# Gated mix of an S5 scan and a SiLU MLP on one core: later columns of the first x rows in two loads, the third block of W1 on ScalarE's queue, the parameter rows on SyncE's queue

## The chip, the cores and the metric

The kernel runs on one core of a Trainium2 chip. The metric is the device time of one execution in microseconds (us). Before the change three executions took 137.16, 136.59 and 137.13 us; their median is 137.13 us. One execution was also taken with the hardware profiler: it took 137.01 us.

## The reference

x has 2048 rows of 448 numbers in bf16, and so has the output. Per row a gate g = sigmoid(sum(x * gate_w)) mixes two branches, `g * a + (1 - g) * b`:

```
a:  Lam_bar = exp(exp(log_dt) * (Lambda_re + 1j*Lambda_im))
    Bu = x @ (((Lam_bar - 1)/Lam)[:, None] * (B_re + 1j*B_im)).T
    h_t = Lam_bar * h_{t-1} + Bu_t                  # 2048 steps
    a = 2 * real(h @ (C_re + 1j*C_im).T) + x * Dskip
b:  b = silu(x @ w1) @ w2                           # 448 -> 1792 -> 448
```

## The kernel before

The 2048 rows of x are read as 1024 pairs, `x2` (line 160): a pair of rows, the even and the odd one, lies in one row of 896 numbers. The work goes by quarters of 512 rows (even or odd, first or second half). The MLP's first product needs x with its columns on the partitions: 448 columns are three blocks of 128 (j = 0, 1, 2) and a rest of 64 (j = 3). W1 lies in `W1E` in the same four blocks. TensorE (PE) runs the MLP's first product into PSUM, ScalarE (ACT) applies SiLU from PSUM to `AT`, and PE runs the second product with W2. Between these, PE makes Bu, VectorE (DVE) runs the scan, and at the end PE applies C.

A small tracker (lines 43 to 148) records every operation with the tiles it reads and writes, derives the semaphore waits, and emits the instructions of each engine in recorded order. So each engine, and each of the two queues that issue DMAs (SyncE's, SP in the profile, and ScalarE's, ACTq), works strictly in the order of the code. All plain loads are issued through one helper, line 226.

The change lies in the start-up, before the steady state:

- **Loads** (lines 275 to 300). Only the first quarter (even rows, first half: 512 pairs in four row blocks k = 0 to 3) has its x brought in plain form, into `XH`, which is a view of the tile `XN`. Its columns 0 to 255 (j = 0, 1) come in four loads of 64 KB, keys XA0 to XA3. Its columns 256 to 511 (j = 2 and the rest) come in one load of 256 KB for all four row blocks, key XB, on ACT's queue (line 284). W1's columns 0 to 767 come by row block: block 0 in two halves, block 1 (192 KB, line 281) and block 2 (192 KB, line 285) on SP's queue. Three parameter rows of 0.9 KB, log_dt, Lambda_re and Lambda_im, go to three partitions of the tile `R` (`ld_row`, line 261); two are on SP's queue and Lambda_im is on ACT's. Then follow the rest of block 3 (`ld_wr`), the other columns of W1, the gate and skip vectors.
- **Transposes by DMA** (lines 307 to 318). SP waits until both `ld_wr` loads have landed (`gE`), and then issues transposing DMAs for the other quarters of x and for B.
- **PE's first work** (lines 484 to 522). After 22 warm-up products PE turns the first quarter itself, 128x128 at a time, against an identity (`turn_x`, line 488); DVE copies the result from PSUM to `XT` (`turned_x`, line 496). The generator `ffn1_first` (line 426) gives the first products (line 432) of six output blocks: all that need j = 0, then j = 1, then j = 2, broken off at fixed places. The order on PE is: turns of j = 0 and 1 for row blocks 0 and 1; products of j = 0; turns of j = 0 and 1 for blocks 2 and 3 among them; three products of j = 1; `mm_cols` (line 468), which turns the parameter rows in `R` into columns; the turns of j = 2; three more products of j = 1; the turns of j = 3; six products of j = 2; then `ffn1_rem` (line 442) with the rest of 64 columns, and after it the pairs of line 364.
- **Parameters**. DVE copies a stripe of `R` (`rd`, line 464), then PE's `mm_cols` result to `PV` (line 514). ACT and DVE form from it dt, the decay magnitude and the angles (lines 551 to 584).
- **Later uses of x**. The gate and the skip product (lines 632 to 647) read the whole of `XH` and wait for all keys in the list `XA`.

Of the kernel before, what the change touches and what calls it, by code (L numbers as in the profile page):

```python
# [150 lines left out]
def gated_mix(nc, A_x, A_Lambda_re, A_Lambda_im, A_B_re, A_B_im, A_C_re, A_C_im, A_log_dt,  # L151
              A_Dskip, B_x, B_w1, B_w2, gate_w, out):
    with ExitStack() as ctx:
        E = ctx.enter_context
        T = Tracker(nc, ctx)

        def sb(name, shape, dtype):
            return E(nc.sbuf_tensor(name, list(shape), dtype))
# [30 lines left out]
        ID = sb("ID", [128, 128], BF16)  # L189
# [31 lines left out]
        ps = E(nc.psum_tensor("ps", [128, 8, 512], F32))  # L221
# [3 lines left out]
        def ld(eng, dst, src, key, group=None):  # L225
            return T.dma(eng, lambda e: e.dma_start(dst, src), writes=[key], group=group)  # L226
# [23 lines left out]
        def row(v):  # L250
            return v.rearrange("(o n) -> o n", o=1)

        XH = XN[:, 0:8 * D].rearrange("p (k c) -> p k c", k=4)
        XA = ["XA0", "XA1", "XA2", "XA3", "XB"]
        FA, FB = 768, 1280
        x0 = x2[0:512, 0:512].rearrange("(k p) c -> p k c", p=128)

        def ld_w(eng, j, f0=0, f1=FA, key=""):
            ld(eng, W1E[:, j, f0:f1], B_w1[j * 128:(j + 1) * 128, f0:f1], f"W1Ej{j}{key}")

        def ld_row(eng, i, v):
            ld(eng, R[i:i + 1, 0:D], row(v), f"R{i}", gR if i < 2 else gR2)
# [5 lines left out]
        def ld_wr(eng, c, later):  # L268
            p = slice(64 * c, 64 * c + 64)
            if later:  # L270
                return ld(eng, W1E[p, 3, 384:896].rearrange("p (n f) -> p n f", n=2),
                          B_w1[384:448, FA:].rearrange("p (n c f) -> p n c f", n=2, c=2)[:, :, c, :], f"W1Es{c}")
            return ld(eng, W1E[p, 3, 0:384], B_w1[384:448, 384 * c:384 * c + 384], f"W1Er{c}")

        for k, eng in enumerate(("sp", "act")):
            ld(eng, XH[:, k, 0:256], x0[:, k, 0:256], XA[k])
        for c, eng in enumerate(("sp", "act")):
            ld_w(eng, 0, 384 * c, 384 * c + 384, c)
        for k, eng in ((2, "sp"), (3, "act")):
            ld(eng, XH[:, k, 0:256], x0[:, k, 0:256], XA[k])  # L280
        ld_w("sp", 1)
        for i, (eng, v) in enumerate((("sp", A_log_dt), ("sp", A_Lambda_re), ("act", A_Lambda_im))):
            ld_row(eng, i, v)
        ld("act", XH[:, :, 256:512], x0[:, :, 256:512], XA[4])
        ld_w("sp", 2)
        gE = [ld_wr(eng, c, False) for c, eng in enumerate(("sp", "act"))]
        ld_w3("sp", 0, 2, FA, FB, "d")
        ld_w3("act", 2, 3, FA, FB, "d")
# [23 lines left out]
        for i, src in enumerate((A_B_re, A_B_im)):  # L312
# [15 lines left out]
             writes=["IOTA"])  # L328
# [128 lines left out]
        def ffn1(c, f0=0, ahead=None):  # L457
            for fb in range(f0, NFB, 2):
                pair(*ffn1_pair(c, fb), last=(c == 3 and fb == NFB - 2))
                if ahead and fb == 8:  # L460
                    ahead()
                yield
# [22 lines left out]
        PB = (6, 7, 6, 7)  # L485
        xp = [ps[:, b, 0:256].bitcast(BF16) for b in PB]

        def turn_x(j, i):
            def mm(pe):
                ins = None  # L490
                for k in (2 * i, 2 * i + 1):
                    ins = pe.transpose(xp[j][:, k * 128:(k + 1) * 128], XH[:, k, j * 128:(j + 1) * 128], ID[:, :])  # L492
                return ins
            T.op("pe", mm, reads=(XA[2 * i:2 * i + 2] if j < 2 else [XA[4]]) + ["ID"], writes=[f"ps{PB[j]}"])

        def turned_x(j, i=None):
            c, key = (slice(0, 512), f"XTe0{j}") if i is None else (slice(256 * i, 256 * i + 256), f"XTe0{j}{i}")
# [2 lines left out]
        for j in range(2):  # L500
            turn_x(j, 0)
            turned_x(j, 0)
        warm(2, 5)
        first = ffn1_first()
        next(first)
        turn_x(0, 1)
        turned_x(0, 1)
        next(first)
        turn_x(1, 1)
        turned_x(1, 1)  # L510
        rd()
# [4 lines left out]
            reads=["pv", "ps7"], writes=["PV"])  # L516
# [30 lines left out]
        def pact(o, a, f, ra, scale=1.0, bias=0.0):  # L547
# [20 lines left out]
            reads=["f2"] + SGN, writes=["f2s"])  # L568
# [55 lines left out]
        def xblock(b):  # L624
            v = XN[:, 4 * b * D:4 * (b + 1) * D].rearrange("p (k c) -> p k c", k=4) if b > 1 else \
                XH[:, :, b * D:(b + 1) * D]
            return v, [*(XA if b < 2 else []), *([f"XN{b // 2}"] if b else [])]

# [12 lines left out]
        def skip():  # L641
            for b in range(4):
# [17 lines left out]
             writes=["BTz"] + BTK[2:4])  # L660
# [486 lines left out]
        f = ffn1(2)  # L1147
# [70 lines left out]
def bass_gated_mix__ssm_conv_s5__dense_activation_silu__prompt_kernel(nc, *args):  # L1218
    gated_mix(nc, *args)
# [28 lines left out]
```

## Time and profile before

| | |
|---|---|
| median of the three runs | 137.13 us (136.59 to 137.16) |
| profiled execution | 137.01 us |
| its span (first to last instruction) | 135.6 us |
| PE busy | 132.3 us, 98% of the span |
| DVE, ACT, POOL busy | 113.8, 93.7, 16.9 us |
| bytes by DMA | 11.95 MB, of them 10.53 MB on SP's queue (q1) and 1.27 MB on ACT's (q10) |

The profile page shows busy time by engine, then the span in 40 slices, the DMA queues, the chain of work that ended last, and groups of instructions by line. PEld is the loading of the stationary matrix, which overlaps PE. SPq and ACTq are the sequencers that issue DMAs. An issue is short; its bytes move later, on 16 DMA engines that both queues share. The views of the trace list single instructions with start and duration in us from the span's start, and after them, in brackets, how long the engine was idle before and what released it.

### The profile page before, as it was taken

The page shows a single profiled execution, that of the slowest core. Times are in us where ns is not written, and L with a number is a line of the kernel's source. Part 1 is how long each engine was busy: PE and PEld are TensorE (multiplying, and loading weights), DVE is VectorE, ACT ScalarE, POOL GpSimd, SP SyncE. Part 2 cuts the span into 40 slices and gives each one's busy share as a digit, 9 for nine tenths or more (in the row PEclk, how much of TensorE's full clock was granted, in tenths as well). Part 3 has the DMA queues.
Part 4 walks back from the last instruction along what each step waited for, and adds up shares of the span by engine and source line. Part 5 has one row for each costly group of instructions (what it writes and reads, how often), then busy time and mean ns, then how long its engine had stood idle before and what let it go on. Part 6 is the DMA issues. An engine that isn't in the chain of part 4 may idle for free.

```text
span 135.6 us, 2631 instructions
## 1 busy us (share of the span) xinstructions
PE 132.3 (98%) x1074; PEld 66.3 (49%) x1075; DVE 113.8 (84%) x150; ACT 93.7 (69%) x146; POOL 16.9 (12%) x32
## 2 busy tenths in 40 slices
PE   7989999999999999999999999999999999999993
PEld 7644444444444555444445544445555555555552
DVE  1358899917699998999999999999999999994554
ACT  0459888899939999778999597797213437879200
POOL 7107758550000000000000000000000000000000
DMA  3999969997899130000122000000000000222123
GB/s 115 255 288 184 156 137 249 172 291 256 234 223 132 36 82 0 0 0 0 42 50 68 5 0 0 0 5 0 0 0 0 0 0 6 100 87 82 68 79 124
DMA packets 24912, 11.95 MB, mean 88 GB/s; under 512 B 16579, under 2 KB 24390, under 8 KB 24902
## 3 DMA queue, kind: packets, MB, share of 16 engines
q1 hardware_dynamic: 22868, 10.53, 34.2%
q10 hardware_dynamic: 2034, 1.27, 3.4%
q8 instruction: 8, 0.13, 0.4%
q14 instruction: 2, 0.02, 0.0%
HBM read 5.51 MB, written 1.84 MB: 54 GB/s over the span
## 4 chain that ended last, share of the span: by engine, by line
PE 92%; DMA 4%; ACTq 1%; DVE 1%; issue 0%
PE ps L364 43%; PE ps L780 16%; PE ps L795 16%; PE ps L1033 15%; DMA XN<-in_A_x_dram 4%; PE ps L432 1%; ACTq L226 1%; DVE TMPS L1057 1%; PE ps L446 1%; PE ps L492 0%
## 5 line engine op out<-in xcount | busy, mean ns | idle before, releaser
L364 PE MATMUL ps<-XT,W1E 64*128 64x512 bf16 x325 | 41.3, 376 | 0.0
L454 ACT ACTIVATE AT<-ps 128x1024 bf16<-128x1024 f32 x28 | 28.2, 1019 | 7.4 <-PE ps L364 7.2
L364 PEld LDWEIGHTS ps<-XT,W1E 64*128 64x128 bf16 x325 | 16.9, 94 | 19.0 <-ACT AT L454 0.3
L364 PE MATMUL ps<-XT,BT 64*128 64x512 bf16 x156 | 22.4, 376 | 0.0
L795 PE MATMUL ps<-W,AT 64*128 64x448 bf16 x224 | 21.5, 349 | 0.0
L780 PE MATMUL ps<-W,AT 128*128 128x448 bf16 x112 | 21.4, 353 | 0.0
L780 PEld LDWEIGHTS ps<-W,AT 128*128 128x128 bf16 x112 | 10.9, 98 | 10.5 <-issue 0.4
L795 PEld LDWEIGHTS ps<-W,AT 64*128 64x128 bf16 x224 | 10.9, 94 | 10.4
L824 ACT ACTIVATE BT<-ps,GT 128x448 bf16<-128x448 f32 x8 | 5.1, 633 | 13.2 <-PE ps L780 13.2
L880 DVE SCALAR_TENSOR_TENSOR HS<-VE,P,ps 128x512 bf16<-128x512 bf16 (+1 forms) x13 | 9.6, 780 | 4.0 <-PE ps L364 4.0
L364 PEld LDWEIGHTS ps<-XT,BT 64*128 64x128 bf16 x156 | 8.1, 94 | 9.4 <-DVE HS L880 0.3
L924 DVE TENSOR_TENSOR_SCAN G<-P,Q 128x1024 f32<-128x1024 f32 (+1 forms) x6 | 11.4, 1922 | 0.0
L1033 PE MATMUL ps<-CO,VE 128*128 128x448 bf16 (+2 forms) x63 | 11.1, 332 | 0.0
L1033 PE MATMUL ps<-CO,HS 128*128 128x448 bf16 x56 | 11.1, 352 | 0.0
L364 PE MATMUL ps<-XR,W1E 64*128 64x512 bf16 x25 | 9.2, 376 | 0.0
L1033 PEld LDWEIGHTS ps<-CO,VE 128*128 128x128 bf16 x63 | 6.0, 98 | 4.8
L1033 PEld LDWEIGHTS ps<-CO,HS 128*128 128x128 bf16 x56 | 5.5, 98 | 5.1
L877 DVE TENSOR_TENSOR Q<-G,COS 128x2048 bf16<-128x2048 f32 (+1 forms) x4 | 7.0, 1756 | 0.1
L877 DVE TENSOR_TENSOR Q<-G,SIN 128x2048 bf16<-128x2048 f32 (+1 forms) x4 | 7.0, 1750 | 0.0
L842 ACT ACTIVATE VE<-ps 128x1024 bf16<-128x1024 f32 x6 | 6.1, 1020 | 1.2 <-PE ps L364 1.2
L844 ACT ACTIVATE ps<-VE,P 128x1024 f32<-128x1024 bf16 x6 | 6.7, 1118 | 0.2
L880 DVE SCALAR_TENSOR_TENSOR VE<-HS,P,FP 128x512 bf16<-128x512 bf16 (+1 forms) x7 | 6.6, 977 | 0.1
(122 smaller groups left out, 181.7 us busy)
## 6 DMA issues: line engine op xcount, KB each, us to landing
W<-in_B_w_dram SPq DMA_DIRECT2D x2, 784.0 KB, 6.3
XN<-in_A_x_dram SPq DMA_DIRECT2D x1, 896.0 KB, 6.1
out_dram<-OT SPq DMA_DIRECT2D x8, 112.0 KB, 1.7
out_dram<-TMPS SPq DMA_DIRECT2D x7, 112.0 KB, 1.7
HS<-HS SPq DMA_DIRECT2D x4, 128.0 KB, 2.3
W1E<-in_B_w_dram SPq DMA_DIRECT2D x2, 192.0 KB, 4.1
XN<-in_A_x_dram SPq DMA_DIRECT2D x1, 384.0 KB, 3.8
XN<-in_A_x_dram ACTq DMA_DIRECT2D x1, 256.0 KB, 4.8
```

Of the source, the lines that this page charges most:

```text
L226: return T.dma(eng, lambda e: e.dma_start(dst, src), writes=[key], group=group)
L364: ins = pe.matmul(ps[:, bank, :], w(p, j), xh(odd, h, j, p), start=start and j == js[0], stop=stop and j == js[-1], skip_group_check=seeded)
L454: T.op("act", lambda e: e.activation(a[:, fb:fb + n, :], ps[:, bank:bank + n, :], AF.Silu), reads=[f"ps{bank + i}" for i in range(n)], wri ...
L780: ins = pe.matmul(ps[:, bank, 0:D], a[:, fb, q * 128:(q + 1) * 128], W2[:, ff(fb), :], start=(first and fb == 0), stop=(fb == NFB - 1), sk ...
L795: ins = pe.matmul(ps[:, bank, 0:D], a[p, fb, q * 128:(q + 1) * 128], W2[p, ff(fb), :], start=(start and fb == 0), stop=(not start and fb = ...
L824: T.op("act", lambda e: e.activation(bs(tile), ps[:, bank, 0:D], AF.Copy, scale=sc), reads=[f"ps{bank}", "GT2" if h else "GRI"], writes=ks)
L842: T.op("act", lambda e: e.activation(VE[:, m:m + 2, hs], ps[:, b[0]:b[0] + 2, :], AF.Copy), reads=[f"ps{i}" for i in b], writes=vs)
L844: T.op("act", lambda e: e.activation(ps[:, o[0]:o[0] + 2, :], VE[:, m:m + 2, hs], AF.Copy, scale=c1("lr", pt)), reads=vs + ["lr"], writes= ...
L877: T.op("dve", lambda e: e.tensor_tensor(o, a, b, op), reads=reads, writes=writes)
L880: T.op("dve", lambda e: e.scalar_tensor_tensor(o, a, s, b, ALU.mult, ALU.add), reads=reads, writes=writes)
L924: T.op("dve", lambda e: e.tensor_tensor_scan(G[:, c, w], rb, Q1[:, c, w], init, ALU.mult, ALU.add), reads=[f"Q1{c}", "rr", f"G{c}"], write ...
L1033: ins = pe.matmul(ps[:, bank, c], state(kt, odd, m), CO[:, m, c], start=False, stop=(m == YB[-1]), skip_group_check=True)
```

## The change

```diff
-        XA = ["XA0", "XA1", "XA2", "XA3", "XB"]
+        XA = ["XA0", "XA1", "XA2", "XA3", "XB0", "XB1"]
...
         ld_w("sp", 1)
-        for i, (eng, v) in enumerate((("sp", A_log_dt), ("sp", A_Lambda_re), ("act", A_Lambda_im))):
-            ld_row(eng, i, v)
-        ld("act", XH[:, :, 256:512], x0[:, :, 256:512], XA[4])
-        ld_w("sp", 2)
+        for i, eng in ((1, "sp"), (0, "act")):
+            ld(eng, XH[:, 2 * i:2 * i + 2, 256:512], x0[:, 2 * i:2 * i + 2, 256:512], XA[4 + i])
+        for i, v in enumerate((A_log_dt, A_Lambda_re, A_Lambda_im)):
+            ld_row("sp", i, v)
+        ld_w("act", 2)
         gE = [ld_wr(eng, c, False) for c, eng in enumerate(("sp", "act"))]
...
-            T.op("pe", mm, reads=(XA[2 * i:2 * i + 2] if j < 2 else [XA[4]]) + ["ID"], writes=[f"ps{PB[j]}"])
+            T.op("pe", mm, reads=(XA[2 * i:2 * i + 2] if j < 2 else [XA[4 + i]]) + ["ID"], writes=[f"ps{PB[j]}"])
```

The load XB of 256 KB becomes XB0 (row blocks 0 and 1, 128 KB, ACT's queue) and XB1 (row blocks 2 and 3, 128 KB, SP's queue). The turns of j = 2 and 3 for row blocks 0 and 1 wait for XB0 alone, those for row blocks 2 and 3 for XB1. W1's block 2 is issued by ACT after XB0, where SP issued it before. Lambda_im's row is issued by SP after the other two rows, where ACT issued it ahead of XB. The same bytes are loaded, and no computing instruction is added or removed. The order of the issues after the six loads that both versions share:

| queue | before | after |
|---|---|---|
| SP | W1 block 1, log_dt, Lambda_re, W1 block 2, `ld_wr` 0, ... | W1 block 1, XB1, log_dt, Lambda_re, Lambda_im, `ld_wr` 0, ... |
| ACT | Lambda_im, XB, `ld_wr` 1, ... | XB0, W1 block 2, `ld_wr` 1, ... |

## The prediction

> **What bounds the kernel now.** I read the page first: PE is busy 98% of the span. A PE-bound kernel gets shorter only where PE is idle, so I went on to the chain that ended last, in order of time. Columns: start, duration in us, what.
>
> ```profile
> 2.21 0.53 ACTq L226
> 2.75 0.03 issue
> 2.78 4.78 DMA XN<-in_A_x_dram
> 7.56 0.05 issue
> 7.61 0.40 PE ps L492 x4
> 8.00 0.05 issue
> 8.05 0.59 PE ps L432 x2
> 8.65 0.22 PE ps L492 x4
> 8.87 1.29 PE ps L432 x6
> 10.17 0.75 PE ps L446 x6
> 10.92 31.76 PE ps L364 x294
> ```
>
> The chain runs through ACT's issues (the 0.53 us one is Lambda_im's row) to the load XB, from 2.78 to 7.56, and from there on through PE to the end. So the turns of j = 2, which wait for XB, set the end, and everything behind them is PE work without a gap. PE's timeline tells how much XB costs:
>
> ```profile
> 5.65 1.53 PE L432 MATMUL ps<-XT,W1E 128*128 128x256 bf16 x9
> 7.01 0.24 PE L471 MATMUL ps<-ID,R 128*128 128x4 bf16 x4
> 7.61 0.40 PE L492 MATMUL ps<-ID,XN 128*128 128x128 bf16 x4 [0.35 <-DMA XN<-in_A_x_dram]
> ```
>
> PE ends the parameter columns (L471) at 7.01 + 0.24 = 7.25 and begins the turns at 7.61. That hole of 0.36 us is all that an earlier XB can give. The waits by engine show the load before it in PE's order, W1's block 1, for which the weight load waits too. The 0.5 us are two waits, of 0.29 us before 4.0 us (first columns of W1) and 0.17 us before the products of j = 1 at 6.35 us:
>
> ```profile
> PEld ps L432 <- DMA W1E<-in_B_w_dram: 0.5, 2, 0.3
> PEld ps L492 <- DMA XN<-in_A_x_dram: 0.4, 1, 0.4
> ```
>
> So W1's block 1 lands at about 6.3 and has no slack: each us that it comes later is a us of PE. XB is the second of two loads that land just when they are needed.
>
> **The change, part by part.** The queues' timelines give the issue costs:
>
> ```profile
> 2.17 0.43 SPq L226 DMA_DIRECT2D W1E<-in_B_w_dram  x1
> 2.65 0.34 SPq L226 DMA_DIRECT2D R<-in_A_log_dt_dram  x1
> 3.03 0.23 SPq L226 DMA_DIRECT2D R<-in_A_Lambda_re_dram  x1
> ...
> 3.30 0.36 SPq L226 DMA_DIRECT2D W1E<-in_B_w_dram  x1
> ```
>
> *Issues on ACT.* Lambda_im's row (0.53 + a gap of 0.04) goes, so XB0 is issued at 2.21 where XB was at 2.78. W1's block 2 follows at about 2.65, and the next load (`ld_wr` 1, 3.21 before) at about 3.1. ACT's later loads and its first activation move forward by 0.1 us, which nothing waits for: ACT's table load begins at 5.11 with ACT idle.
>
> *Issues on SP.* After W1's block 1 come XB1 at 2.65 (0.42, as an XN load takes on SP at 1.71), then the rows at 3.11, 3.49 and 3.76 (0.34 and twice 0.23, gaps 0.04), then `ld_wr` 0 at 4.03 where it was at 3.70. So five loads behind it (`ld_wr` 0, the next columns of W1 and so on) are issued 0.33 us later. Of these the first needed is the 256 KB block (issued at 4.31, 5.3 us to landing, so 9.6); PE needs it for line 364 at 10.5. It would come at 9.6 to 9.95, PE would need it at 10.15 or later: 0, with 0.2 us of cover left. SP's transposes wait for both `ld_wr` loads, until 8.08 now. Their first product, x's second half, lands at about 13.9 and is used by PE at about 16.15; 0.33 us later costs 0, the cover is 2.2 us.
>
> *The rows.* All three were landed when DVE copied the stripe of R (L465) at 6.06, since that copy starts right behind DVE's work before it. Lambda_im, issued at 2.21, took at most 3.85 us therefore; the trace's landing events put the rows at 1.8 to 2.1 us after their issue. The last row is now issued at 3.76: it lands between 5.9 (2.1 us) and 7.6 (3.85 us). PE loads L471's weights at 6.80, so about 6.5 costs nothing, and every us after that holds PE at L471 by as much. I take 5.9, the measured row: 0. The upper end would hold PE 1.1 us, less the 0.36 us of hole that it fills.
>
> *XB0 and XB1.* XB0 is issued 0.57 us earlier and has half the bytes, so it comes well ahead of XB1. XB1 stands behind W1's block 1 on SP and is the one that decides. It cannot land before that block (6.3). The load that stood in this place of SP's queue was W1's block 2, 192 KB, issued at 3.30; in a window of the DMA view it took 4.2 us to land, so 7.5. Going from 6.3 to 7.5 for 192 KB, 128 KB would come at 6.3 + 1.2 x 128/192 = 7.1. But the engines are shared and full by then:
>
> ```profile
> 6.30:7.30 1.00, 0.96 (x9) 0.46 (x7) 0.00 (x1) 0.30 (x2) 0.00 (x0) 1.00 1.02 309
> ```
>
> The last two columns are the DMA engines' busy share, 1.02, and 309 GB/s. From 6.3 to 7.56 they move about 390 KB. If ACT's block 2 (192 KB) and the remainder of the loads behind it take their turns ahead of XB1's 128 KB, XB1 lands at 7.6 as XB does now. So the ends are 7.1 and 7.6, and I take the middle, 7.35. Then PE's hole is 0.1 us instead of 0.36 us: **-0.2 us**. With 7.25 or less it would be the whole -0.36 us.
>
> *A rule of the Trainium skill speaks against it.* The engines full at 1.02 are the row. The page "DMA: Bandwidth & Descriptors", section "Rules for kernel authors", says that spreading loads over several issuing engines brings no bandwidth, because all run on the same 16 DMA engines; only issue time is saved. By the rule alone, with the engines full, XB1 would land where XB does and the sum would be 0; this trace shows the engines full only from about 5 us on.
>
> *W1's block 1.* Its bytes now meet XB0's from the start, 0.57 us earlier than XB's before. Between 3.5 and 5.0 the DMA view shows 200 GB/s on average, against 304 GB/s between 5.0 and 7.6, so there is room, and I take 0. The bound on the other side is a load of W1 on a queue under full load: 4.4 to 5.6 us from issue to landing in the rows of the DMA view, against 4.1 us now:
>
> ```profile
> W1E<-in_B_w_dram SPq DMA_DIRECT2D x1, 256.0 KB, 5.3
> ...
> W1E<-in_B_w_dram SPq DMA_DIRECT2D x1, 48.0 KB, 4.4
> ```
>
> *W1's block 2* moves to ACT, issued at 2.65 instead of 3.30; it is first needed at 8.7, and lands by 7.6 at the latest: 0.
>
> *Behind the turns.* Does the gain reach the end? DVE's copy of the turned x, dt's angle product, ACT's magnitude and table load, and the first SiLU (10.53) all follow the turns and move with them. PV comes from L471 and stays at 7.30; dt is ready at 7.7, while DVE wants it at 8.0 even after the gain. Then PE stays dense; its list of waits has no other entry after the start than XB's 0.35 us.
>
> **The sum.** 137.01 us (span 135.6, 1.4 around it) - 0.2 us = **136.8 us**. The median of the three runs, 137.13 us, is 0.12 above the profiled execution; their scatter, 0.57 us, is larger than the gain. What a measurement of this kernel can tell from no change is about 0.5%, 0.69 us.
>
> **Rivals.**
> 1. *The transfer is no earlier* (the change doesn't do what it is for): XB1 lands at 7.5 to 7.6, behind block 2 on the shared engines. For it: 1.02 busy. Against: half of XB is 0.57 us earlier in a stretch with room. 137.0 us.
> 2. *Slower: W1's block 1 is late.* XB0 and then block 2 take their share of the same engines while block 1 moves. PE stands before the products of j = 1. The hole at XB is then filled, so it costs from a landing at about 6.35 + 0.36 = 6.7 on, and 0.5% from 7.4 on. With the 5.3 us of the row above it lands at 2.17 + 5.3 = 7.47: +1.1 - 0.36 = +0.76, 137.8 us. Against: the room before 5 us.
> 3. *The rows are late* behind XB1: up to 7.6, +1.1 - 0.36, again 137.8 us at the worst, 137.2 us with half of that. Against: 2.1 us measured, behind W1's block 1 on the same queue.
> 4. *Both loads earlier*: the room before 5 us is filled, and block 1 gains as well. PE's two waits, 0.36 + 0.17, all go: 136.5 us. More than 0.5% needs scatter on top.
>
> **How the numbers follow.** Forecast (XB1 between 6.7 and 7.45, -0.1 to -0.36, so 136.65 to 136.9): 0.5. No earlier: 0.22. W1 late: 0.13. Rows late: 0.08. Both earlier: 0.07. The forecast, the first rival and the mild ends of the others lie within 0.5%: 0.79. Faster by more: 0.07, from the fourth. Slower by more: 0.14, 0.09 of the second and 0.05 of the third. The range goes from 136.4 (fourth case, 136.5, and the scatter) to 137.6 (most of the second and third).
>
> **What would show it.** Right: in the chain the load of XN ends at 7.2 to 7.45; PE's idle time before L492 falls from 0.35 to some 0.1 us, and L446 begins some 0.2 us earlier than 10.10; W1E's wait before L432 stays at 0.5 in total. Wrong: L432 waits for W1E by 0.5 us more, DVE's L465 waits for R, or an idle stretch appears before L364 at 10.5.

## The result, and the profile after

The changed kernel is slower: 138.10 us median of 16 executions (136.63 to 138.31) against 136.77 us of the kernel before in as many, ratio 1.0085, 95% interval 1.0069 to 1.0101 (the ratios here are estimated over all executions, and differ a little from the quotient of the two medians). Its profiled execution took 138.23 us with a span of 136.7 us, 1.1 us more span than before.

The chain of work that ended last, in order of time, of the changed kernel (start, duration in us, what; its lines are those of before plus one):

```profile
3.79 4.43 DMA R<-in_A_Lambda_im_dram
8.22 0.04 DVEq L146
8.26 0.05 issue
8.31 0.18 DVE R L466
8.48 0.14 issue
8.62 0.24 PE ps L472 x4
8.86 0.24 PE ps L493 x4
...
11.27 0.76 PE ps L447 x6
12.03 31.76 PE ps L365 x294
```

Where XB stood in the chain before, Lambda_im's row stands now: 0.9 KB, issued at 3.79, landed 4.43 us later, at 8.22. PE's turns of j = 2 (L493) come right behind the parameter columns (L472), so XB0 and XB1 had been there for a while. From L447 on everything is 1.1 us later than before (11.20 against 10.10 in PE's timeline), and the steady part (31.76 us in both) is unchanged. The loss is made between 7 and 8.7 us and nothing is added or given back later.

PE's timeline of the changed kernel, and its engine busy times in the hole (the first number is the window's length; then busy us of PE, PEld, DVE, ACT and POOL; the last three are clock, DMA share, GB/s):

```profile
6.42 0.82 PE L433 MATMUL ps<-XT,W1E 128*128 128x512 bf16 x3 [0.49 <-DMA W1E<-in_B_w_dram]
8.62 0.24 PE L472 MATMUL ps<-ID,R 128*128 128x4 bf16 x4 [1.38 <-DVE R L466]
8.72 0.38 PE L493 MATMUL ps<-ID,XN 128*128 128x128 bf16 x4
```

```profile
7.24:8.62 1.38, 0.01 (x1) 0.03 (x1) 0.17 (x1) 0.00 (x0) 0.00 (x0) 1.00 1.01 316
```

PE is idle for 1.38 us; the copy of the stripe (L466) that released it waited for the rows, and the DMA engines were full (1.01, 316 GB/s) all that time, with loads that PE was not waiting for. Before, L471 ran at 7.01 and PE waited 0.35 us for XB instead.

The issues on SP's queue in the changed kernel, and the landing of the loads in question in the DMA view (last column: us from issue to landing):

```profile
2.64 0.43 SPq L226 DMA_DIRECT2D XN<-in_A_x_dram  x1
3.12 0.37 SPq L226 DMA_DIRECT2D R<-in_A_log_dt_dram  x1
3.53 0.22 SPq L226 DMA_DIRECT2D R<-in_A_Lambda_re_dram  x1
3.79 0.52 SPq L226 DMA_DIRECT2D R<-in_A_Lambda_im_dram  x1
```

```profile
W1E<-in_B_w_dram SPq DMA_DIRECT2D x1, 192.0 KB, 4.2
...
XN<-in_A_x_dram ACTq DMA_DIRECT2D x1, 128.0 KB, 4.6
XN<-in_A_x_dram SPq DMA_DIRECT2D x1, 128.0 KB, 4.9
```

The issue times of XB1 and of the rows are those of the forecast. Behind them Lambda_im's issue took 0.52 us where 0.23 was forecast, so `ld_wr` 0 went out at 4.36 and not at 4.03. By the trace's landing events XB0 landed at 6.82 and XB1 at 7.53; XB landed at 7.56 before. So without the wait for the rows the turns of row blocks 0 and 1 would not have waited at all in this execution, and those of row blocks 2 and 3 could have begun at about 7.58; a gain of some 0.15 us, by an estimate from these numbers (the third turn began at 7.73 before).

### The profile page after: what moved, and what is told of

It is laid out like the page before. It is cut to its first block, busy times and chain, and to the rows that moved or that the text cites. A ratio compares the mean times of both kernels' runs of the same rounds, so it can differ in the third digit from the quotient of the medians.

```text
span 136.7 us, 2633 instructions
## 1 busy us (share of the span) xinstructions
PE 131.9 (96%) x1075; PEld 65.8 (48%) x1075; DVE 113.9 (83%) x150; ACT 93.8 (69%) x146; POOL 16.9 (12%) x32
## 4 chain that ended last, share of the span: by engine, by line
PE 92%; DMA 3%; SPq 2%; DVE 1%; issue 0%; DVEq 0%
PE ps L365 43%; PE ps L781 16%; PE ps L796 15%; PE ps L1034 15%; DMA R<-in_A_Lambda_im_dram 3%; SPq L226 2%; PE ps L433 1%; DVE TMPS L1058 1%; PE ps L447 1%; PE ps L493 0%; PE ps L472 0%; DVE R L466 0%; DVEq L146 0%
```

## The experiments

Three theories were set against each other. *Place*: the rows wait behind XB1's bytes in SP's queue. *Time*: they are issued later, into a stretch in which any small load takes long. *Weight*: block 2 on ACT's queue holds them up. All ratios are to the kernel before, run beside them.

**Rows ahead of XB1**, in the changed kernel.

```diff
         ld_w("sp", 1)
+        for i, v in enumerate((A_log_dt, A_Lambda_re, A_Lambda_im)):
+            ld_row("sp", i, v)
         for i, eng in ((1, "sp"), (0, "act")):
             ld(eng, XH[:, 2 * i:2 * i + 2, 256:512], x0[:, 2 * i:2 * i + 2, 256:512], XA[4 + i])
-        for i, v in enumerate((A_log_dt, A_Lambda_re, A_Lambda_im)):
-            ld_row("sp", i, v)
```

> The changed kernel with one order turned round on SP's queue: W1's block 1, the three parameter rows, then XB1 (the changed kernel has XB1 ahead of the rows). Place theory (the rows wait in the queue behind XB1's bytes): the rows land by about 5.8 us, as in the kernel before; the 1.4 us that PE waited before the parameter columns are gone; XB1 is issued about 1.1 us later (3.8 instead of 2.64) and lands at 7.5 to 8.0, so PE waits there 0.3 to 0.7 us; about 136.9 to 137.3 us. Time theory (the rows are only issued later, and any small load issued in this stretch takes 4.4 us): issued at 2.65 to 3.3 they land at 7.0 to 7.7, PE waits 0.5 to 0.8 us: 137.5 us. Weight theory (block 2 on ACT's queue holds SP's loads up): as the changed kernel, 138 us.

137.26 us, ratio 1.0033 (1.0013 to 1.0054). Turning the order round takes about 0.5 of the 0.85 per cent away, and leaves about 0.3; XB1 is now issued at 3.58 instead of 2.64. Its profiled execution, 138.24 us, is the longest of its twelve (PE got its first x at 4.01 instead of 3.12), so the ratio counts here and not the profile's length. In it the last row landed at 6.27, nearer to the place theory's 5.8 than to the time theory's 7.0 to 7.7, and DVE's copy of R did not wait for it:

```profile
6.97 0.16 DVE L466 COPY R<-R 3x64 bf16<-3x64 bf16 x1
```

**Lambda_im's row alone moved**, in the kernel before.

```diff
-        for i, (eng, v) in enumerate((("sp", A_log_dt), ("sp", A_Lambda_re), ("act", A_Lambda_im))):
+        for i, (eng, v) in enumerate((("sp", A_log_dt), ("sp", A_Lambda_re), ("sp", A_Lambda_im))):
             ld_row(eng, i, v)
```

> The kernel before with one part of the change alone: Lambda_im's row goes from ACT's queue to SP's, behind the other two rows; XB stays whole on ACT's queue and is issued 0.57 us earlier, block 2 of W1 stays on SP's. Place theory: with only W1's block 1 ahead of them all rows land by 5.8 us, no wait; XB lands 0.1 to 0.57 us earlier: 136.4 to 136.8 us, 0.1 to 0.4 us less than before. Time theory: Lambda_im, issued at 3.3, takes 4.4 us, lands at 7.7; PE waits 0.7 us less what it waits for XB now: 137.2 us. Weight theory: no change from before but for XB, 136.6 us.

137.87 us, ratio 1.0083 (1.0054 to 1.0112): with no XB1 ahead of the rows, this one move costs as much as the whole change. So a place behind XB1 is not the only way to lose this much; that it is harmless does not follow, because most of the loss is not the rows' here. In the profile the copy of R waits until 7.28, and PE waits 0.49 us for it, which costs 0.1 us against before, as the wait for XB is gone. Then a second load is late, which costs 0.5 us: the last 64 KB of W1's rest on SP, issued at 5.59, which takes 6.35 us.

```profile
10.84 0.81 PE L364 MATMUL ps<-XT,W1E 64*128 64x512 bf16 x6
11.99 0.39 PE L364 MATMUL ps<-XT,W1E 64*128 64x512 bf16 x1 [0.34 <-DMA W1E<-in_B_w_dram]
```

Before, the same product ran at 11.41 without a wait.

**Block 2 back on SP's queue**, in the changed kernel, behind the rows.

```diff
-        ld_w("act", 2)
+        ld_w("sp", 2)
```

> The changed kernel with W1's block 2 back on SP's queue, behind the rows. Place theory: the rows still stand behind XB1; they land at 7.2 to 8.0 and the time is as that of the changed kernel, 137.7 to 138.1 us. Time theory: the same. Weight theory: without block 2's heavy packets beside them XB1 lands by 6.8 and the rows by 7.0, PE waits 0.2 us at most: 136.7 us.

138.44 us, ratio 1.0122 (1.0094 to 1.0150). Without block 2 beside them the kernel is slower, not faster, so moving block 2 back does not win the loss back. Its weight is not nothing, though: the last row landed at 7.38 here and XB1 at 6.99, against 8.22 and 7.53 in the changed kernel. PE waits for the rows (0.3 us) and then for the last W1 columns (0.4 us, landed at 12.17), in a profile that is the shortest of its six executions (137.69 us):

```profile
7.78 0.24 PE L472 MATMUL ps<-ID,R 128*128 128x4 bf16 x4 [0.33 <-DVE R L466]
12.22 0.39 PE L365 MATMUL ps<-XT,W1E 64*128 64x512 bf16 x1 [0.39 <-DMA W1E<-in_B_w_dram]
```

**All rows on GpSimd's queue**, in the changed kernel, issued behind the identity matrix.

```diff
-        for i, v in enumerate((A_log_dt, A_Lambda_re, A_Lambda_im)):
-            ld_row("sp", i, v)
...
+        for i, v in enumerate((A_log_dt, A_Lambda_re, A_Lambda_im)):
+            ld_row("pool", i, v)
```

> The changed kernel with the three rows on GpSimd's queue, issued after its identity matrix at about 1.4 us, so on neither queue. All theories: the rows are early (by about 5 us), PE's wait for them goes. What is left is the change without the rows' place: XB1 lands at 7.2 to 7.4 as it did in the changed kernel, PE's wait before the turns of j = 2 is 0 to 0.2 us instead of 0.35 us, about 136.5 us (0.2 to 0.3 us less than before). If XB1's share is not earlier, 136.8 us. If the generation of the loads on GpSimd takes longer than 5 us, PE waits again.

136.93 us, ratio 1.0003 (0.9982 to 1.0023). The loss is gone, and the hoped-for gain does not show (0.15% would lie within the interval). Its profile is the shortest of its twelve executions (136.13 us); there XB1 landed 4.3 us after its issue, at 6.95, the copy of R ran at 6.34, and PE hardly waited at L472 or L493 (0.14 us of weight load for XB1). Its DMA view has a number for small loads on a queue of their own:

```profile
R<-in_A_log_dt_dram POOLq DMA_DIRECT2D x1, 0.9 KB, 2.9
R<-in_A_Lambda_re_dram POOLq DMA_DIRECT2D x1, 0.9 KB, 3.2
R<-in_A_Lambda_im_dram POOLq DMA_DIRECT2D x1, 0.9 KB, 3.5
```

No big load stands ahead of the rows on their own queue here, and yet each takes longer than the one before it.

**The third row on SP, but XB kept at its issue time**, in the kernel before: ACT loads the row as well, to a tile that nobody reads then.

```diff
-        for i, (eng, v) in enumerate((("sp", A_log_dt), ("sp", A_Lambda_re), ("act", A_Lambda_im))):
-            ld_row(eng, i, v)
+        ld("act", OT[0:1, 0, :], row(A_Lambda_im), "OT0")
+        for i, v in enumerate((A_log_dt, A_Lambda_re, A_Lambda_im)):
+            ld_row("sp", i, v)
```

> The kernel before with Lambda_im's row issued by SP as third row, and a second load of the same row, to a tile nobody reads then, in the row's old place on ACT's queue, so that XB keeps its issue at 2.78. SP-side theory (a third row in series on SP, and 0.5 us of SP's issue time put ahead of all its later loads): as the run with one row moved, 137.5 to 137.9 us. Head-start theory (ACT's loads, 0.57 us earlier, take engine time from what SP's queue holds): as before, 136.8 to 137.0 us.

136.83 us, ratio 1.0015 (0.9994 to 1.0037): no loss to speak of.

**XB 0.57 us earlier, but no third row on SP**, in the kernel before: Lambda_im goes to GpSimd's queue, behind the identity matrix.

```diff
-        for i, (eng, v) in enumerate((("sp", A_log_dt), ("sp", A_Lambda_re), ("act", A_Lambda_im))):
-            ld_row(eng, i, v)
+        for i, v in enumerate((A_log_dt, A_Lambda_re)):
+            ld_row("sp", i, v)
...
+        ld_row("pool", 2, A_Lambda_im)
```

> The kernel before with Lambda_im's row on GpSimd's queue (after its identity matrix): ACT's queue has lost the row, so XB is issued 0.57 us earlier, and SP's queue is as before. SP-side theory: no loss; XB lands 0.1 to 0.5 us earlier, 136.5 to 136.9 us. Head-start theory: the two rows on SP and SP's W1 loads are late, 137.4 to 137.9 us.

136.88 us, ratio 1.0019 (0.9999 to 1.0039): none that is clear of the interval either. So neither the third row on SP nor ACT's head start costs much alone, and both together cost 0.83%. That is what slack does. In these two profiles the copy of R ran at 6.91 and 6.94 instead of 6.06, and PE, which wants the rows at about 6.6 to 6.8, lost little (in the second it was waiting for W1's block 1 until 6.87 anyway); with both it ran at 7.28, and in the changed kernel at 8.31. The last W1 columns on SP landed at 10.85 and 10.88 instead of 9.90, ahead of their products at 11.12 and 11.41; with both they landed at 11.94, and PE waited.

**One row behind XB1**, in the changed kernel; log_dt and Lambda_re go to GpSimd's queue.

```diff
-        for i, v in enumerate((A_log_dt, A_Lambda_re, A_Lambda_im)):
-            ld_row("sp", i, v)
+        ld_row("sp", 2, A_Lambda_im)
...
+        for i, v in enumerate((A_log_dt, A_Lambda_re)):
+            ld_row("pool", i, v)
```

> The changed kernel with log_dt and Lambda_re on GpSimd's queue; only Lambda_im is left on SP's queue behind XB1. If the rows' lateness is XB1's bytes ahead of them plus one turn per row in series, Lambda_im lands right behind XB1, at about 7.5 instead of 8.1, PE waits about 0.6 us less: 137.3 us. If a row behind XB1 is late whatever stands between, it lands at 8.1: 138.0 us. If the place behind XB1 doesn't matter: as with all rows on GpSimd's queue, 136.9 us.

137.08 us, ratio 1.0026 (1.0004 to 1.0049). In the chain the row is the bound again:

```profile
3.12 4.21 DMA R<-in_A_Lambda_im_dram
...
7.36 0.05 issue
7.41 0.18 DVE R L467
```

It takes 4.21 us, nearly the 4.43 us of the changed kernel, and lands at 7.33 instead of 8.22 mainly because it is issued 0.67 us earlier, with no other row ahead of it. XB1 landed at 7.12 in this profile, the row 0.21 us behind it, as the first of the three expectations has it.

**The queues as changed, the rows idle**: SP loads the three rows in the same place to a tile that nobody reads then; the used rows come by GpSimd's queue.

```diff
-            ld_row("sp", i, v)
+            ld("sp", OT[i:i + 1, i, :], row(v), f"OT{i}")
...
+        for i, v in enumerate((A_log_dt, A_Lambda_re, A_Lambda_im)):
+            ld_row("pool", i, v)
```

> The changed kernel with its queues as they are, and the wait taken away: SP issues the same three rows in the same place, but to a tile that nobody reads then; the rows that are used come by GpSimd's queue. Rows theory (the whole loss is PE's wait for the three rows): as with all rows on GpSimd's queue, 136.8 to 137.0 us. Crowding theory (the rows' issues on SP, 1.2 us in all, push SP's later W1 columns back, and these make PE wait whatever the rows do): 137.5 us or more.

137.31 us, ratio 1.0033 (1.0013 to 1.0054). The same traffic without PE's wait for SP's rows costs 0.33% instead of 0.85%: that wait is worth about 0.5%, 0.7 us. The time lies between the two expectations. In the profile, the shortest of its twelve (136.81 us), the used rows are in the chain that ended last, though PE's wait for them is short now:

```profile
2.72 4.07 DMA R<-in_A_Lambda_im_dram
...
7.19 0.24 PE ps L474 x4
```

**The same for the kernel with Lambda_im alone moved**: XB whole on ACT's queue, block 2 on SP's, and this edit to the kernel before.

```diff
-        for i, (eng, v) in enumerate((("sp", A_log_dt), ("sp", A_Lambda_re), ("act", A_Lambda_im))):
-            ld_row(eng, i, v)
+        for i, v in enumerate((A_log_dt, A_Lambda_re, A_Lambda_im)):
+            ld("sp", OT[i:i + 1, i, :], row(v), f"OT{i}")
...
+        for i, v in enumerate((A_log_dt, A_Lambda_re, A_Lambda_im)):
+            ld_row("pool", i, v)
```

> The same for the kernel with Lambda_im's row alone moved: XB whole on ACT's queue at 2.21, three rows on SP that nobody reads, the used rows by GpSimd's queue. In the profile of that kernel PE waited 0.1 us more for rows than before for XB, and 0.5 us for the last W1 columns of the rest (landed at 11.94 instead of 9.9). Rows theory: 136.6 to 136.9 us. Crowding theory: the wait for the last W1 columns stays, 137.3 to 137.6 us.

137.53 us, ratio 1.0063 (1.0031 to 1.0095). Here the wait for the rows is a small part, and the late W1 columns the larger:

```profile
5.50 6.13 DMA W1E<-in_B_w_dram
11.63 0.05 issue
11.68 0.39 PE ps L366
```

So the one-row kernel and the changed kernel lose about the same by different waits. With W1's block 2 still on SP and ACT's loads early, three rows on SP go with late last columns; with block 2 on ACT these come in time and the rows are late. No run moves those columns alone in the one-row kernel, so their share there is read from the chain.

**The changed kernel once more.**

> The changed kernel once more, beside the others on one chip. Rows theory: the same wait in a second profile, DVE's copy of R at 8 us or later, PE's columns after it, 138.0 us. If the first profile was one of many: PE's wait lies elsewhere, at W1's block 1 or XB.

138.03 us, ratio 1.0077 (1.0049 to 1.0104). The second profile shows the same chain, DVE's copy at 8.11 and PE's columns at 8.43:

```profile
3.81 4.21 DMA R<-in_A_Lambda_im_dram
```

**W1's block 1 in halves**, with all rows on GpSimd's queue: the half that PE uses first on SP, the other on ACT behind XB0; and the same with Lambda_im on ACT in its old place.

```diff
-        ld_w("sp", 1)
+        ld_w("sp", 1, 0, 384, 0)
...
+        ld_w("act", 1, 384, 768, 1)
         ld_w("act", 2)
```

> All rows on GpSimd's queue, and W1's block 1 in two halves: the half that PE uses first stays on SP's queue, the other goes to ACT's queue behind XB0, ahead of block 2; PE waits for each half by itself. If W1's block 1 is what holds PE once the rows are out of the way, the first half (96 KB instead of 192 KB) lands at about 5.5 instead of 6.3, the products of j = 1 begin when those of j = 0 end, XB1 comes 0.3 us earlier, and the time is 136.4 us, 0.4 to 0.5 us below before. If the late engines set every landing alike, 136.9 us.

> W1's block 1 in halves as before, log_dt and Lambda_re on GpSimd's queue, Lambda_im back on ACT's queue in its old place, so XB0 0.57 us later. Rows theory: the last row lands before 6 us instead of 6.8, PE's 0.3 us for rows goes; XB1 on SP decides: 136.1 to 136.4 us. If the rows on GpSimd's queue were not what PE waited for in most executions: 136.35 us, as with all three there.

The first: 136.35 us, ratio 0.9980 (0.9955 to 1.0004), the only kernel below before, but its interval touches no change. The second: 137.13 us, ratio 1.0016 (1.0001 to 1.0031). Its rows are in time (copy at 5.77), but block 2 now stands behind the row, XB0 and the half block on ACT's queue, and PE waits 0.78 us for it at 9.08. A version that surely beats both was not found.

**Where the rest of the loss lies.** The idle rows still cost 0.33%. In the four kernels p1 to p4 the transposing DMAs are replaced by plain loads; p4 also moves the last 64 KB of W1's rest from SP to ACT.

```diff
-            return T.dma("sp", lambda e: e.dma_start_transpose(dst, src), reads=reads,
+            return T.dma("sp", lambda e: e.dma_start(dst, plain), reads=reads,
...
-        for c, eng in enumerate(("sp", "act")):
-            ld_wr(eng, c, True)
+        for c in (1, 0):
+            ld_wr("act", c, True)
```

Here `plain` is as many bytes of x or B_re as the tile holds; so these kernels leave the transposition out, and all that follows from it holds other numbers than the reference's. The second part is p4's alone.

> The kernel before with the transposition by DMA left out: the second quarter, the odd rows, B and C are filled by plain loads of the same tile sizes, so their contents are not the reference's. It is the yardstick for the three kernels beside it. Both theories: PE stays the bound from 8 us on, so about as before, 136.3 to 137.0 us.

> The changed kernel with the same plain loads in place of the transposing DMAs (contents not the reference's). Rows theory: 1.0 to 1.3 us more than the kernel before in this form, with PE's wait for the rows in the profile.

> The changed kernel with idle rows on SP and the used rows by GpSimd's queue, with the same plain loads (contents not the reference's). Crowding theory: 0.3 to 0.6 us more than the kernel before in this form, as with the transposing DMAs. Rows theory alone: no more than 0.2 us more.

> The same with the last 64 KB of W1's rest on ACT's queue instead of SP's (contents not the reference's). If SP's late load is what the idle rows cost: back to the kernel before in this form, within 0.2 us. If it is not: as with idle rows.

| kernel | median us | ratio to before (95%) |
|---|---|---|
| p1, as before | 136.96 | 1.0009 (0.9987 to 1.0031) |
| p2, as changed | 137.95 | 1.0071 (1.0042 to 1.0101) |
| p3, idle rows | 137.24 | 1.0027 (1.0006 to 1.0048) |
| p4, idle rows, last load on ACT | 137.02 | 1.0022 (0.9997 to 1.0048) |

p2 repeats the change's loss over p1 (0.6%) and p3 the share of the wait (0.4% from p2 to p3). p4 is as p3 within the intervals, so the late last load is not shown to be the cause of the rest here. In the profiles of p3 and p4 the used rows on GpSimd's queue took 4.5 us and landed at 7.24 and 7.17.

## Why the prediction was wrong

**The step that failed** is the rows: "I take 5.9, the measured row: 0." The sum took 2.1 us from issue to landing, which the rows had in the one profile before, for rows that are now issued 0.5 to 1.6 us later and behind XB1. The last one took 4.43 us and landed at 8.22; the prediction's own upper end was 3.85 us, 7.6. PE began the parameter columns at 8.62 instead of 7.01, +1.61; 0.50 of that is won back, because the turns now follow the columns' start by 0.10 us instead of 0.60 (XB has long landed), and 1.11 is left, which is what L493 shows: 8.72 against 7.61. That is the third rival, with its mechanism and place, at a higher price than its worst, 137.8 us; it had a chance of 0.08.

Why the rows took so long, by the runs. The traces' records of single DMA packets tell when a row's 896 bytes moved, which takes 0.04 us. For the last row on SP's queue (us from the span's start):

| profile | issued | bytes moved | landed | big load just ahead on SP, landed |
|---|---|---|---|---|
| before | 3.03 | 4.72 | 5.11 | W1 block 1, 6.31 |
| p1, as before | 3.00 | 5.50 | 6.07 | W1 block 1, 6.00 |
| rows ahead of XB1 | 3.28 | 5.62 | 6.27 | W1 block 1, 6.29 |
| Lambda_im's row alone moved | 3.29 | 6.36 | 7.19 | W1 block 1, 6.24 |
| block 2 back on SP | 3.88 | 6.40 | 7.38 | XB1, 6.99 |
| one row behind XB1 | 3.12 | 6.51 | 7.33 | XB1, 7.12 |
| changed | 3.79 | 7.02 | 8.22 | XB1, 7.53 |
| changed, again | 3.81 | 6.78 | 8.02 | XB1, 7.65 |

Fifteen profiles have rows on SP's queue. In fourteen the last of them landed between 0.01 us before and 1.2 us after the big load ahead of it; in the profile before alone it was 1.2 us ahead of that load. So the 2.1 us that the prediction trusted were one draw, and the fastest: p1, with the same loads up to there, has 3.1 us. Place carries the larger part: behind XB1 the bytes moved at 6.78 and 7.02, with the order turned round at 5.62. Half a microsecond of that difference is time, the later issue. The engines' load has a part too: in the run without block 2 on ACT the bytes waited 2.52 us for their turn, in the two profiles of the changed kernel 2.97 and 3.23 us. No run separates the three exactly. The engines are full from 5 to 8 us in both kernels (busy share 0.94 to 1.01 before, 0.95 to 1.00 after), and a load of 0.9 KB then takes as long as one of 192 KB (4.2 us). A queue of its own does not save the rows from this: the third row took 3.5 to 4.5 us on GpSimd's. The Trainium skill's page "DMA: Bandwidth & Descriptors", section "Queues, rings and completion order", says that a DMA's completion mark lands only after all earlier writes of the same DMA engine, over all queues; the 0.4 to 1.5 us from the last row's bytes to its landing in these profiles agree with it, though no run here isolates it. The same page's section "Anatomy of one DMA — SWDGE (gpsimd) path" gives a fixed cost of about 2 us for a load that GpSimd issues; the rows on GpSimd's queue took 2.8 to 4.5 us, and the measurement decides.

**The forecast's own gain** is not shown either. XB1 was put at 7.35; it landed at 7.53 in the first profile, and between 6.45 and 7.83 in the eleven profiles that issue it at about 2.64. XB, issued at 2.78, landed at 7.56 in the profile that the prediction read, but at 6.63 in p1 and at 6.60 where ACT loads the row as well; in those two PE did not wait for it, so the hole of 0.36 us was one draw as well. The end of the range, 7.6, "behind block 2 on the shared engines", was nearly right for the first profile, which was the first rival. The room before 5 us that spoke against it was read from 200 GB/s; the engines' busy share in that stretch, 3.5 to 5.0, was 0.91 in the same profile. With the rows out of the way the kernel is at 1.0003 (0.9982 to 1.0023). The rule that the prediction cites from the skill's section "Rules for kernel authors", that a second issuing queue brings no bandwidth, gave 0 and agrees with that.

**Right**: W1's block 1 is not later (6.38 against 6.31). PE does wait 0.49 us for it in the changed kernel's profile, but because the products of j = 0 were done earlier there (at 5.94); those of j = 1 end at 7.24 instead of 7.18. Block 2 on ACT is in time, the issue times up to the rows are as forecast, and the loads behind the rows (four plain ones, where the prediction counts five) and the transposes cost nothing in the changed kernel. SP's last W1 columns, which the prediction did not look at (it priced the first block behind the rows only), landed at 10.45 there and at 10.68 with idle rows, and PE did not wait. This goes with block 2 off SP or ACT's loads late: of the three kernels with three used rows and block 2 on SP, the columns landed at 11.94 and 12.17 in two (the one-row kernel and the one with block 2 back), where PE waited for them, and at 10.85 in the third, where XB kept its issue time.

**Shown and open.** Shown: the wait for the rows carries about 0.5% of the 0.85% (idle rows against the changed kernel, twice: 1.0085 to 1.0033, and 1.0071 to 1.0027), and the order on SP's queue alone gives as much back (1.0033). Open: the remaining 0.2 to 0.3%. With idle rows in the changed kernel the used ones, on GpSimd's queue, took 4.1 and 4.5 us (p3), against 3.5 us with all rows there and no idle ones, and PE waited 0.16 us for them in the first, so a part may be the same wait again; but with block 1 in halves they took 4.1 us, too, without a loss. The last W1 load was not shown to be it (p4). Neither was measured apart. How much of the rows' lateness is ACT's earlier loads is open as well: no run keeps the rows behind XB1 with ACT's loads at their old times.

## What to carry to other kernels

In these runs a small load that gates something came when its bytes got their turn among what was issued before it, not by its size nor by its issue cost: when big loads are moved forward, look first at which small one now stands behind them, and when it is wanted. A landing time from one profile is one draw; price a small load behind a big one as landing about when the big one does. Two moves that each eat a part of one slack can cost nothing apart and 0.8% together.

## What the runs showed of the hardware

- 0.9 KB took from 1.8 to 4.5 us to land, on three different queues: 1.8 to 2.1 us on ACT's behind 64 KB loads, 2.1 to 4.5 us on SP's behind loads of 128 or 192 KB, 2.8 to 4.5 us on GpSimd's, which held nothing else.
- GpSimd spent 0.74 and twice 0.49 us to issue the three rows, against 0.22 to 0.52 on SP, and the work behind them (IOTA) began at 3.21 instead of 1.43, which nothing waited for.
- Executions of one kernel differ by over 1 us (136.63 to 138.31 for the changed kernel), and the profiles put such differences into the first 10 us: the span of p1 is 0.79 us shorter than that of the kernel before, and PE comes to its first product with the rest of 64 columns (L446 before) at 9.31 instead of 10.10. The shortest of twelve in one kernel, 136.13, and the longest of twelve in another, 138.24, were each the profiled ones; the medians are 136.93 and 137.26. A ratio of many executions has to stand beside every profile here.
